# Loading q in runs for two of six token groups, decaying it as it leaves PSUM, and a new order of steps, in a linear-attention and MLP kernel

## The chip, the cores and the metric

The kernel runs on one core of one Trainium2 chip. The metric is the device time of one execution in microseconds (us), lower is better. The five engines of a core are named as in the profile: PE is TensorE (with PEld for its weight loads), DVE is VectorE, ACT is ScalarE, POOL is GpSimd and SP is SyncE. Each engine executes its own instructions in order and waits on semaphores for the others.

## The reference

Two functions follow each other. The first is causal linear attention with a decay for each head; the second is an MLP with the activation h * tanh(softplus(h)), named Mish in the kernel. Cut to what matters (`pos` counts 0 to 63 inside a block of 64):

```python
# q, k, v: (4, 8, 768, 64) float32; lam: (8,)
Dmask = where(rel >= 0, lam ** rel, 0)              # rel = pos_i - pos_j
for each block of 64 positions:
    intra = ((q @ k.T) * Dmask) @ v
    inter = (q * lam ** (pos + 1)) @ kv_state
    out = intra + inter
    kv_state = lam ** 64 * kv_state + (k * lam ** (63 - pos)).T @ v
x = out as (3072, 512)
h = x @ w_in                                        # (512, 2048)
return (h * tanh(softplus(h))) @ w_out              # (2048, 512)
```

## The kernel before

**Tiling.** The kernel takes 128 positions as one block instead of 64, which gives the same function. There are six groups of positions (n = 0 to 5) and in each four batches (b = 0 to 3); steps are named by n and b. The decay is split into a factor for the key's position (held in the masks `dv` and in `lkt`) and one for the query's position, `lqi`, which multiplies the output of a block at its end: (q k^T masked) v and q times the state are both linear in q, so that it may stand at either place. In group 0 the state is zero and only the first part exists.

**Steps.** For each n and b: `lk`, `lq`, `lv` load k, q and v as float16 by a DMA that POOL issues (L155), with positions on partitions, so that one load consists of 8 heads by 128 rows of 64 numbers. In groups 0 and 1 `pk` and `pq` transpose k and q on PE against the identity `ident` (L313) and DVE or ACT copies the result out of PSUM: `kk` (DVE) and `ek` (ACT) for k, `eq` (DVE) and `ea` (ACT) for q. In groups 2 to 5 the transposes are DMAs of SP (`tk`, `tq`). `sc` computes the scores (L386) into two banks, `mk` multiplies them with the mask (DVE, L392), `yo` or `yt` multiplies with v (L403), `yi` adds q times the state (L418), and `xd` multiplies the output with `lqi` and writes it to `xt`, the input of the MLP (DVE, L423). `kp` (POOL) or `kd` (DVE) makes the decayed keys `ktil`, `pv` and `ra` the new state, `wu` or `wd` its decay.

The MLP of groups 0 and partly 1 is computed directly: `u` (one quarter of w_in by one batch, L610) and `uu` (L627) are matmuls, `mu` and `mv` the activation. All other work of the MLP is by a seven-product scheme: `p` (L573) and `o` (L667) are its matmuls, `ws`, `wt`, `ts` and `gs` its sums of operands (DVE), `ca`, `cc`, `ad`, `c2`, `m` and `oa`, `oc`, `od`, `e` the ways out of PSUM, `st` the stores. `wi` and `wo` load quarters of the two weight matrices.

**Constants at the start.** `ir` is an iota on POOL (`rel`); from it DVE makes `ek` and `eq` (step `ik`), `ei` (`ie`), the identity (`di`) and the causal mask (`dk`). `pl` spreads lam on PE, ACT takes its logarithm (`an`) and `lkt` (`ak`); `dp` copies the logarithms by head pairs (`lnp`, DVE), `dq` and `ai` make `lqi` (DVE, ACT), `al` makes `lbm`. `fk` and `ck` bring the first k, group 0 and batch 0, by SP and ACT. `zz.m` is a filler of PE: matmuls of zeros over m x 128 columns.

**What sets the order.** Nothing is scheduled by rules: the table `ORDER` (L15 to L93) lists all steps, and each engine receives its instructions in that order. What follows @ in a step are the PSUM banks (0 to 7) that it takes. A step that takes a bank waits until the last step that had it is through. The last loop of the kernel (L772) executes the table.

A path for q in "runs" is in the code already, for the groups in `IN_RUNS`, which is empty (L128): `lq` then loads 8 neighbouring rows to one partition, and `pq_` picks the rows apart in its transpose (L327 to L332). Tiles of q, k and v have 8 buffers each (L154).

Of the kernel before, what the change touches and what calls it, by code (L numbers as in the profile page):

```python
# [15 lines left out]
fk lk.1.1 lk.0.1 lq.1.2 lq.0.1 lk.0.3 lq.1.1 lq.0.3 ir lk.0.2 lq.0.0 lv.0.0 lv.0.1 lq.0.2 lv.0.3 z0 ll la  # L16
zz.12@0 pl@1 an ik ak dp dk di zz.57@0 pk.1.1@1 ie dv.1 dq kk.1.1 zz.4@0 pq.1.1@2 pk.0.1@3 kk.0.1 pq.0.1@4
pq.1.2@5 pk.0.3@1 ea.0.1 zz.5@0 pk.0.2@3 sc.0.1@4,6 dv.0 kd.0.2 ek.0.3 ea.1.2 ea.1.1 pq.0.3@1 eq.0.3 zz.7@0
sc.0.3@5,2 mk.0.1.1 mk.0.3.1 ck pk.0.0@1 ek.0.0 pq.0.0@7 ea.0.0 zz.10@0 pq.0.2@1 sc.1.1@7,6 mk.0.3.0 kk.0.2
# [1 line left out]
xd.0.1 wi.1 lv.0.2 wi.0 lk.1.0 wi.2 lq.1.0 lk.1.2 kp.0.1 xd.0.3 mk.0.2.0 mk.0.2.1 zz.4@0 u.0.1.1@2 u.0.1.3@3
lm mu.0.1.1 mu.0.1.3 wi.3 kp.0.3 yo.0.2@1 pv.0.2@4 pv.0.3@2 pv.0.1@3 lk.1.3 lq.1.3 xd.0.0 ra.0.2 xd.0.2
mk.1.1.0 mk.1.1.1 ra.0.1 ra.0.3 kd.0.0 lv.1.0 kp.1.0 lv.1.1 lv.1.2 u.0.1.0@5 u.0.1.2@4 uu.0.0.0.0@1
uu.0.0.0.1@3 uu.0.0.1.0@2 pk.1.0@7 uu.0.0.1.1@6 mv.0.0.0.0 mv.0.0.1.1 mv.0.0.1.0 mv.0.0.0.1 mu.0.1.2
uu.0.2.0.1@1 uu.0.2.1.1@6 mv.0.2.1.1 pk.1.2@2 pq.1.0@3 uu.0.2.0.0@4 mv.0.2.0.1 kk.1.2 mv.0.2.0.0 mu.0.1.0
# [780 lines left out]
```

## Time and profile before

| | us |
|---|---|
| time, median of 3 runs | 200.76 (200.47 to 201.5) |
| the profiled execution | 200.44 |
| its span in the profile | 198.7 |
| PE busy in the span | 188.9 |
| DVE busy | 152.6 |
| POOL busy | 96.4 |
| ACT busy | 94.3 |

The span runs from the first to the last instruction; 1.7 us of the execution lie around it. A busy PE is not one at its peak, since fillers and matmuls in a pipeline count as well. In a timeline row stand the start, the duration, the engine, the line, the operation with what it writes and reads, and the number of instructions that the row takes together; in brackets the idle time before it and what ended it. In a row of the chain of waits stand the start, the duration and what the chain went through. In a row of a group stand the busy time in us and the mean of one in ns, then the idle time before it.

### The profile page before, as it was taken

How to read it: one execution, taken by the hardware profiler on the slowest of the kernel's cores; microseconds unless marked ns; L12 is line 12 of the kernel's file. 1: busy time of each engine (PE TensorE's matmuls, PEld its weight loads, DVE VectorE, ACT ScalarE, POOL GpSimd, SP SyncE). 2: the span in 40 equal slices, each digit the busy share in tenths (PEclk: the TensorE clock that was granted, in tenths of full speed). 3: DMA queues.
4: the chain of work that ended last, by engine and by line, in shares of the span. 5: the costliest groups of instructions: out<-in, count | busy, mean ns of one | idle time of the engine just before them, and what ended most of it. 6: DMA issues, size and time to landing. Idle time of an engine off the chain costs nothing.

```text
span 198.7 us, 5683 instructions
## 1 busy us (share of the span) xinstructions
PE 188.9 (95%) x2398; PEld 160.3 (81%) x2398; DVE 152.6 (77%) x298; ACT 94.3 (47%) x174; POOL 96.4 (49%) x110
## 2 busy tenths in 40 slices
PE   8597999999999998999999999999999999999992
PEld 3264897888888887888888888888888888888881
DVE  0395936999997999859999676999759997686521
ACT  2066227537455131387731659612758236575410
POOL 7999989900990796709930489801342000000000
PEclk9999999999999999999999999999999999999998
DMA  8999999999597299999999369997929104201044
GB/s 89 143 141 175 200 182 159 205 205 150 87 93 90 59 168 167 160 170 112 176 167 60 93 137 133 189 171 153 93 48 143 45 0 139 79 0 56 0 158 162
DMA packets 103228, 24.63 MB, mean 124 GB/s; under 512 B 92834, under 2 KB 103202, under 8 KB 103202
## 3 DMA queue, kind: packets, MB, share of 16 engines
q0 software_dynamic: 78064, 13.51, 88.5%
q1 hardware_dynamic: 24992, 10.69, 25.1%
q8 instruction: 19, 0.31, 0.7%
q14 instruction: 7, 0.06, 0.1%
q10 hardware_dynamic: 146, 0.07, 0.1%
HBM read 27.26 MB, written 6.29 MB: 169 GB/s over the span
## 4 chain that ended last, share of the span: by engine, by line
PE 78%; DVE 10%; POOL 5%; DMA 3%; issue 1%; ACT 1%; POOLq 0%
PE b L667 35%; PE b L573 25%; PE b L627 5%; PE b L403 3%; PE b L386 3%; DMA vn<-in_v_dram 3%; DVE hs L473 3%; POOL qn L155 3%; PE b L418 2%; PE b L610 2%; POOL kn L155 2%; PE b L430 2%; DVE wt L473 1%; DVE ws L473 1%; POOL vn L155 1%
## 5 line engine op out<-in xcount | busy, mean ns | idle before, releaser
L667 PEld LDWEIGHTS <-hs 128*128 128x128 f16 x384 | 37.2, 98 | 4.9 <-issue 0.2
L602 ACT ACTIVATE hsg<-b 128x512 f16<-128x512 f32 x54 | 31.2, 596 | 12.3 <-PE b L573 12.1
L667 PE MATMUL b<-wt,hs 128*128 128x256 f16 x288 | 36.4, 273 | 0.2 <-ACT b L676 0.2
L392 DVE TENSOR_TENSOR sb<-b,dv 128x512 f16<-128x512 f32 x48 | 30.5, 684 | 3.4 <-PE b L386 3.3
L573 PEld LDWEIGHTS <-ws 128*128 128x128 f16 x288 | 28.1, 98 | 3.3
L667 PEld LDWEIGHTS <-hsg 128*128 128x128 f16 x288 | 27.8, 98 | 3.6
L573 PE MATMUL b<-xs,ws 128*128 128x256 f16 x216 | 30.0, 273 | 0.0
L359 POOL TENSOR_TENSOR ktil<-kn,lkt 128x512 f16<-128x512 f16 x17 | 20.7, 1218 | 17.6 <-DMA kn<-in_k_dram 15.7
L667 PE MATMUL b<-wout,hsg 128*128 128x256 f16 x192 | 24.3, 273 | 0.0
L443 POOL TENSOR_TENSOR w<-raw,lbm 128x256 f16<-128x256 f32 x9 | 7.5, 837 | 33.7 <-DVE raw L439 33.7
L573 PEld LDWEIGHTS <-win 128*128 128x128 f16 x216 | 20.9, 98 | 2.6
L155 POOL DMA_DIRECT2D vn<-in_v_dram x24 | 21.9, 923 | 1.3 <-DMA win<-in_moe_w_in_dram 1.1
L155 POOL DMA_DIRECT2D qn<-in_q_dram x24 | 22.1, 934 | 0.1
L155 POOL DMA_DIRECT2D kn<-in_k_dram x23 | 21.3, 939 | 0.8 <-POOLq L790 0.8
L707 ACT ACTIVATE osb<-b 128x512 f32<-128x512 f32 x12 | 7.2, 596 | 28.5 <-PE b L667 28.5
L573 PE MATMUL b<-xt,win 128*128 128x256 f16 x144 | 20.1, 273 | 0.0
L470 DVE TENSOR_TENSOR b<-b,p 128x512 f32<-128x512 f32 x18 | 12.5, 697 | 9.4 <-PE b L573 4.6
L627 PE MATMUL b<-xt,win 128*128 128x256 f16 x160 | 19.1, 273 | 0.0
L627 PEld LDWEIGHTS <-win 128*128 128x128 f16 x160 | 15.3, 98 | 1.9
L634 ACT ACTIVATE hsg<-b 128x512 f16<-128x512 f32 x20 | 11.4, 606 | 11.3 <-PE b L627 11.2
L423 DVE TENSOR_TENSOR xt<-b,lqi 128x512 f16<-128x512 f32 x24 | 15.7, 685 | 1.2 <-PE b L418 1.1
L470 DVE TENSOR_TENSOR c<-b,p 128x512 f32<-128x512 f32 x18 | 12.3, 686 | 5.1 <-PE b L573 5.0
(78 smaller groups left out, 284.7 us busy)
## 6 DMA issues: line engine op xcount, KB each, us to landing
out_dram<-osb SPq DMA_DIRECT2D x23, 256.0 KB, 3.0
qn<-in_q_dram POOLq DMA_DIRECT2D x24, 128.0 KB, 5.7
vn<-in_v_dram POOLq DMA_DIRECT2D x24, 128.0 KB, 4.9
kn<-in_k_dram POOLq DMA_DIRECT2D x23, 128.0 KB, 6.4
win<-in_moe_w_in_dram POOLq DMA_DIRECT2D x4, 512.0 KB, 9.9
wout<-in_moe_w_out_dram POOLq DMA_DIRECT2D x4, 512.0 KB, 9.6
osb<-in_k_dram SPq DMA_DIRECT2D x1, 256.0 KB, 3.0
kraw<-kn SPq DMA_TRANSPOSE x16, 2.5
```

Source lines behind the costliest of these rows:

```text
L155: nc.gpsimd.dma_start(out=to[n, b], in_=rows(t, n, b))
L359: engine.tensor_tensor(out=ktil[n, b], in0=kn[n, b], in1=bc(lkt, 2, D), op=ALU.mult)
L392: nc.vector.tensor_tensor(out=sb[n, b, t], in0=pS[n, b][t], in1=dv[:, t], op=ALU.mult)
L423: nc.vector.tensor_tensor(out=xts(n, b), in0=pO.pop((n, b)), in1=lqi, op=ALU.mult)
L443: nc.gpsimd.tensor_tensor(out=wst[b], in0=raw.pop((n, b)), in1=lbm, op=ALU.mult)
L470: nc.vector.tensor_tensor(out=o, in0=a, in1=b, op=ALU.add)
L473: nc.vector.tensor_tensor(out=o, in0=a, in1=b, op=ALU.subtract)
L573: nc.tensor.matmul(t[:, mi, :], w_half(i, s, mi, kc), x_half(n, i, kc), start=(i in (1, 5) and mi == 0 and kc == 0), stop=(mi == 1 and kc ...
L602: nc.scalar.activation(hidden(n, col - 1, row - 1)[:, 2 * s : 2 * s + 2], src, AF.Mish)
L627: nc.tensor.matmul(ph[n, w, h, f0][:, f, :], win[:, kc, ni * 128 : (ni + 1) * 128], xt[n][:, kc, h * HT : (h + 1) * HT], start=(f == 0 and ...
L634: nc.scalar.activation(hidden(n, h, w // 2)[:, f : f + 2], ph.pop((n, w, h, f0)), AF.Mish)
L667: nc.tensor.matmul(t[:, tb, :], g_half(n, i, ki, tb), o_half(i, ki), start=(i in (1, 5) and tb == 0 and ki == 0), stop=(tb == 1 and ki == ...
```

## The change

Four things are changed together.

1. `IN_RUNS` becomes (0, 1): the eight loads of q for groups 0 and 1 go in runs, 128 partitions of 8 neighbouring rows each, and their eight `pq` become 16 matmuls of 64 columns each into a float32 bank, instead of 4 transposes of 128 columns into a float16 one.
2. A new step `es` replaces the copy of q in group 0: DVE multiplies q with `lqi` as it takes it from PSUM. `lqi` must be there before the scores of group 0.
3. `xa` replaces `xd` in group 0: ACT copies the output from PSUM to `xt`. (A step `xc` that copies on DVE is defined and not used.)
4. The table `ORDER` is new from end to end. Among the kinds of steps, all copies of k in groups 0 and 1 are now `ek` (ACT; before, five of eight were `kk`), `kd` stands six times instead of three and `kp` 14 times instead of 17, `wu` 11 times instead of 9 and `wd` 5 instead of 7, `ea` three times instead of six and `eq` once instead of twice. The products of the MLP are the same in number.

```diff
-fk lk.1.1 lk.0.1 lq.1.2 lq.0.1 lk.0.3 lq.1.1 lq.0.3 ir lk.0.2 lq.0.0 lv.0.0 lv.0.1 lq.0.2 lv.0.3 z0 ll la
-zz.12@0 pl@1 an ik ak dp dk di zz.57@0 pk.1.1@1 ie dv.1 dq kk.1.1 zz.4@0 pq.1.1@2 pk.0.1@3 kk.0.1 pq.0.1@4
...
+fk lq.0.1 lk.1.1 lq.1.2 lk.0.3 lq.0.0 lk.1.0 lq.0.3 ir lk.0.1 lv.0.0 lk.1.2 lq.0.2 lk.0.2 lq.1.0 lv.0.3 ll la
+wi.1 lv.0.2 lq.1.1 lv.0.1 z0 zz.12@0 pl@1 an dp ik ie di dq dk ak ck zz.41@0 pk.0.3@1 kd.1.0 dv.1 zz.13@0
...
-    IN_RUNS = ()
+    IN_RUNS = (0, 1)
...
+    @step
+    def es(n, b):
+        nc.vector.tensor_tensor(out=turned(qraw, "qraw", n, b), in0=pq.pop((n, b)), in1=lqi, op=ALU.mult)
...
+    @step
+    def xa(n, b):
+        nc.scalar.activation(xts(n, b), pO.pop((n, b)), AF.Copy)
```

The first place is POOL's queue from its first load on. `kn`, `qn`, `vn` are tiles of k, q and v (a number tells one tile from the next), and the last figures are the shape that is written. Before:

```order
L155 DMA kn_97<-in_k_dram 128x8x64
L155 DMA kn_99<-in_k_dram 128x8x64
L155 DMA qn_101<-in_q_dram 128x8x64
L155 DMA qn_103<-in_q_dram 128x8x64
L155 DMA kn_105<-in_k_dram 128x8x64
L155 DMA qn_107<-in_q_dram 128x8x64
L155 DMA qn_109<-in_q_dram 128x8x64
L226 ISA
L226 IOTA rel_71 128x128
L155 DMA kn_112<-in_k_dram 128x8x64
```

And with the change:

```order
L171 DMA qn_97<-in_q_dram 128x1x512
L155 DMA kn_99<-in_k_dram 128x8x64
L171 DMA qn_101<-in_q_dram 128x1x512
L155 DMA kn_103<-in_k_dram 128x8x64
L171 DMA qn_105<-in_q_dram 128x1x512
L155 DMA kn_107<-in_k_dram 128x8x64
L171 DMA qn_109<-in_q_dram 128x1x512
L226 ISA
L226 IOTA rel_71 128x128
L155 DMA kn_112<-in_k_dram 128x8x64
```

Seven loads stand ahead of the iota in both; four of them are now loads in runs, before none was.

The second place is VectorE from the making of lqi on. `b` with a number is a PSUM bank, `sb` a masked score, `dv` the mask, `lnp` the logarithms of lam. Before:

```order
L286 TENSOR_TENSOR lqi_80<-ei_73,lnp_79 128x512
L347 COPY kraw_166<-b1_158 128x512
L347 COPY kraw_180<-b3_175 128x512
L266 TENSOR_TENSOR dv_77<-maskT_72,lkt_78 128x512
L359 TENSOR_TENSOR ktil_226<-kn_112,lkt_78 128x512
L335 COPY qraw_239<-b1_234 128x512
L392 TENSOR_TENSOR sb_264<-b6_208,dv_77 128x512
L392 TENSOR_TENSOR sb_266<-b2_247,dv_77 128x512
L392 TENSOR_TENSOR sb_312<-b5_246,dv_77 128x512
```

And with the change, from the first es on, up to the mask behind which the bank of the last transpose ahead of the first u (bank 2) is free:

```order
L360 TENSOR_TENSOR qraw_223<-b3_187,lqi_80 128x512
L364 TENSOR_TENSOR ktil_276<-kn_103,lkt_78 128x512
L397 TENSOR_TENSOR sb_278<-b3_230,dv_77 128x512
L266 TENSOR_TENSOR dv_77<-maskT_72,lkt_78 128x512
L397 TENSOR_TENSOR sb_281<-b2_229,dv_77 128x512
L360 TENSOR_TENSOR qraw_300<-b6_259,lqi_80 128x512
L360 TENSOR_TENSOR qraw_319<-b5_302,lqi_80 128x512
L360 TENSOR_TENSOR qraw_383<-b3_327,lqi_80 128x512
L397 TENSOR_TENSOR sb_424<-b5_365,dv_77 128x512
L397 TENSOR_TENSOR sb_426<-b7_348,dv_77 128x512
L397 TENSOR_TENSOR sb_428<-b2_366,dv_77 128x512
```

The copies of k and q have left VectorE here, and four products with lqi stand ahead of the masks of batches 0, 2 and 1.

The third place is ScalarE up to the first outputs of group 0. Before:

```order
L306 ACTIVATE kn_268<-osb_95 128x512
L343 ACTIVATE kraw_275<-b1_270 128x512
L355 ACTIVATE qraw_282<-b7_277 128x512
L278 ACTIVATE lbm_81<-lnp_79 128x256
L290 ACTIVATE lqi_80<-lqi_80 128x512
L355 ACTIVATE qraw_353<-b1_289 128x512
L223 ACT_TABLE_LOAD
```

And with the change:

```order
L306 ACTIVATE kn_153<-osb_95 128x512
L343 ACTIVATE kraw_204<-b1_167 128x512
L343 ACTIVATE kraw_220<-b2_180 128x512
L290 ACTIVATE lqi_80<-lqi_80 128x512
L278 ACTIVATE lbm_81<-lnp_79 128x256
L223 ACT_TABLE_LOAD
L343 ACTIVATE kraw_292<-b5_249 128x512
```

The exponential for lqi now stands behind two copies of k, ahead of it stood four copies of q and two of k (four of these rows are above the piece of before).

More of the change, by code (lines that the diff above doesn't have):

```diff
@@ L21 @@
[L21 to L25, printed above, removed]
@@ L91 @@
[L91 to L92 removed]
+fk lq.0.1 lk.1.1 lq.1.2 lk.0.3 lq.0.0 lk.1.0 lq.0.3 ir lk.0.1 lv.0.0 lk.1.2 lq.0.2 lk.0.2 lq.1.0 lv.0.3 ll la
+wi.1 lv.0.2 lq.1.1 lv.0.1 z0 zz.12@0 pl@1 an dp ik ie di dq dk ak ck zz.41@0 pk.0.3@1 kd.1.0 dv.1 zz.13@0
+pk.1.0@2 zz.4@0 pq.0.3@3 ek.0.3 pk.1.1@1 zz.3@0 pk.0.1@4 ek.1.0 ai es.0.3 zz.6@0 sc.0.3@2,3 al lm pk.0.0@5
+zz.10@0 pq.0.2@6 kd.0.3 mk.0.3.1 dv.0 mk.0.3.0 zz.6@0 pk.0.2@7 ek.0.0 ek.0.2 ek.1.1 ek.0.1 es.0.2 pq.0.0@5
@@ new lines @@
+mk.1.1.0 kd.1.2 uu.0.0.0.1@4 uu.0.0.0.0@2 uu.0.0.1.1@5 uu.0.0.1.0@6 mv.0.0.0.1 mv.0.0.0.0 mu.0.1.1 mv.0.0.1.0
+mv.0.0.1.1 uu.0.2.1.0@4 uu.0.2.1.1@2 pq.1.3@7 pk.1.3@6 mk.1.2.1 ek.1.3 mu.0.1.2 mv.0.2.1.1 uu.0.2.0.0@1
+mv.0.2.1.0 eq.1.3 yt.1.0@7 yt.1.1@6 yi.1.0 sc.1.3@5,3 yi.1.1 pv.1.0@2 xd.1.0 xd.1.1 wo.1 wo.0 lq.2.1 lk.2.3
+wo.3 gs.0.1.0.4 gs.0.3.0.4 ra.1.0 mk.1.3.0 mk.1.3.1 ws.1.1 ws.2.1 kp.1.1 kd.1.3 wo.2 lk.2.1 lq.2.0
+uu.0.2.0.1@4 uu.1.2.0.0@7 uu.1.0.0.0@6 uu.0.3.0.1@2 uu.0.3.0.0@5 uu.0.3.1.1@3 mv.1.0.0.0 mv.0.2.0.0 mv.0.3.0.1
@@ new lines @@
+mv.1.2.0.0 mv.0.3.0.0 yt.1.2@6 pv.1.3@1 yt.1.3@2 yi.1.2 yi.1.3 uu.0.3.1.0@7 p.1.3.1@5 xd.1.2 xd.1.3 ts.1.1
+ra.1.3 ws.3.1 ts.1.2 ts.1.3 ca.1.3@6 mv.0.3.1.0 mv.0.2.0.1 wt.1.0 ws.4.1 wt.1.1 uu.1.0.1.0@2 uu.1.0.0.1@1
+mv.1.0.1.0 p.1.2.5@7 cc.1.2 p.1.2.1@4 uu.1.0.1.1@2 p.1.3.5@7 lk.2.0 lq.2.2 lk.2.2 lv.2.1 kp.2.1 lq.2.3 tk.2.0
+ca.1.2@0 mv.0.3.1.1 gs.0.1.4.8 p.1.2.6 mv.1.0.0.1 uu.1.2.1.1@3 mv.1.2.1.1 mv.1.0.1.1 cc.1.3 uu.1.2.0.1@1
+mv.1.2.0.1 p.1.3.2 p.1.3.6 p.1.2.2 m.1.2.11 gs.0.2.0.4 o.0.1.0@3 uu.1.2.1.0@2 m.1.3.11 mv.1.2.1.0 ws.1.0
@@ new lines @@
+p.2.3.3 sc.3.1@4,0 p.2.3.7 gs.2.1.0.2 m.2.1.21 m.2.3.12 ad.2.2@3 p.2.2.3 m.2.2.12 m.2.1.22 o.2.1.0@6 wu.2.2
+lq.3.0 gs.2.2.0.2 p.2.2.7 gs.2.4.0.2 c2.2.3 e.1.22 kp.3.2 c2.2.2 gs.2.1.2.4 m.2.3.22 m.2.2.22 mk.3.1.0
+mk.3.1.1 o.2.1.1 p.2.3.4 o.1.4.0 p.2.2.4 oa.2@5 m.2.2.21 o.1.4.1 m.2.3.21 pv.3.1@3 yt.3.1@4 tq.3.0 tq.3.2
+gs.2.3.0.2 gs.2.1.6.8 gs.2.1.4.6 gs.2.3.4.6 gs.2.2.6.8 kp.3.0 lk.3.3 wu.2.1 kp.3.3 sc.3.0@0,2 yi.3.1
+gs.2.2.4.6 ra.3.1 gs.2.3.6.8 gs.2.2.2.4 gs.2.4.6.8 mk.3.0.0 mk.3.0.1 wd.3.1 xd.3.1 gs.2.4.4.6 st.0.22 tk.3.3
@@ L93 @@
+gs.5.3.4.6 gs.5.4.2.4 oc.5 o.5.2.0 od.5@7 gs.5.4.6.8 ed.4.21 gs.5.4.4.6 o.5.7.0 st.4.12 st.3.21 st.4.21
+st.4.22 o.5.3.0 o.5.7.1 o.5.3.1 o.5.2.1 e.5.22 o.5.4.0 o.5.4.1 ed.5.210 ex.5 st.5.22 e.5.12 e.5.11 ey.5 sy.5
+st.5.12 st.5.11 st.5.210 sx.5
 """
@@ L423, in xd, with xc @@
         nc.vector.tensor_tensor(out=xts(n, b), in0=pO.pop((n, b)), in1=lqi, op=ALU.mult)
+    @step
+    def xc(n, b):
+        nc.vector.tensor_copy(xts(n, b), pO.pop((n, b)))
+    @step
+    def xa(n, b):
+        nc.scalar.activation(xts(n, b), pO.pop((n, b)), AF.Copy)
     @step
```

125 lines of the change are left out of this document (55 added, 70 removed).

## The prediction

> **What bounds the kernel now.** I read the page first, for which engine is full and where, then the table of windows, then the chain of waits and the timeline of the first 21 us.
>
> ```profile
> span 198.7 us, 5683 instructions
> PE 188.9 (95%) x2398; PEld 160.3 (81%) x2398; DVE 152.6 (77%) x298; ACT 94.3 (47%) x174; POOL 96.4 (49%) x110
> PE   8597999999999998999999999999999999999992
> PEclk9999999999999999999999999999999999999998
> ...
> 0.00:20.00 20.00, 15.12 (x181) 8.24 (x183) 9.93 (x24) 8.12 (x14) 18.93 (x27) 1.00 1.70 137
> 20.00:195.03 175.03, 173.75 (x2221) 152.04 (x2219) 142.41 (x274) 85.89 (x159) 77.52 (x84) 1.00 1.10 122
> 195.03:198.70 3.67, 0.00 (x0) 0.00 (x0) 0.29 (x1) 0.28 (x1) 0.00 (x0) 0.78 0.48 162
> ```
>
> In a row of windows stand the length, then the busy time of PE, PEld, DVE, ACT and POOL, then the granted clock. TensorE is the bound, but only from about 20 us: from there to its last matmul (195.03) it is busy 173.75 of 175.03 us, so that it idles 1.3 us in all. Before 20 us its 15.1 us are largely dummy matmuls of zz and single small steps, while POOL is busy 18.9 of 20. So the end of the kernel is the moment at which TensorE gets real work without a break, plus the work left then, plus a tail that the change leaves as it is. The prediction is about the first of these three, and then about the second.
>
> The break-free stretch begins with the first u. What released it:
>
> ```profile
> 12.09 5.55 DMA vn<-in_v_dram
> 17.68 0.41 PE b L403 x8
> 18.49 0.69 DVE sb L392
> ...
> 12.09 0.98 POOL L155 DMA_DIRECT2D vn<-in_v_dram  x1
> 12.95 0.87 POOL L184 DMA_DIRECT2D win<-in_moe_w_in_dram  x1
> 13.69 1.01 POOL L155 DMA_DIRECT2D vn<-in_v_dram  x1
> ...
> 19.75 1.29 DVE L423 TENSOR_TENSOR xt<-b,lqi 128x512 f16<-128x512 f32 x2
> 20.49 1.95 PE L610 MATMUL b<-xt,win 128*128 128x128 f16 x32
> ...
> L184 POOL DMA_DIRECT2D win<-in_moe_w_in_dram x1: 868/868/868, 13.0 to 13.0; - x1
> ...
> DMA to landing us min/median/max: 7.2/7.2/7.2
> ```
>
> Two things end together at u (20.49): the chain load of v, yo, scores, mask, yo, xd (19.75 + 0.69 = 20.44), and the first quarter of win, issued at 12.95 and landed 7.2 us later, at 20.15. Both hang on POOL's queue of loads, so an earlier start needs both earlier.
>
> **The change part by part.** *The loads of q.* A plain load has 1024 pieces (8 heads by 128 rows, from the code), a load in runs 128, a quarter of win 512.
>
> ```profile
> 3.17 1.75 POOL qn L155 x2
> ...
> 7.55 0.33 POOL L226 IOTA rel<- 128x128 f32 x1
> 7.74 0.96 POOL L155 DMA_DIRECT2D kn<-in_k_dram  x1
> ...
> DMA to landing us min/median/max: 3.8/3.9/4.0
> ```
>
> Plain loads leave POOL 0.875 us apart, the one of win is followed after 13.69 - 12.95 = 0.74 us. A line through these two gives 0.64 us for 128 pieces. Bounds: 0.11 us if time went by pieces alone (an eighth of 0.875), and 0.875 if it did not depend on them. I take 0.64, nearest to the row with the fewest pieces. Ahead of the first win there are now 14 loads instead of 13, eight plain and six in runs: 1.26 + 8 x 0.875 + 6 x 0.64 + 0.34 for the iota = 12.4 us instead of 12.95. The first loads land 3.9 us after their issue, the v of 12.09 took 5.55: by then 1.6 us of backlog had gathered, and win's 7.2 us contain it. Without it win lands at 12.4 + 5.6 = 18.0, with it at 19.6. Pieces fall from 13,312 to 8,960 ahead of win while bytes rise by one load, so I take the lower end with a small remainder, 18.2.
>
> *The constants and the first scores.* The iota is now behind seven loads of which four are in runs: 1.26 + 3 x 0.875 + 4 x 0.64 = 6.4 instead of 7.55.
>
> ```profile
> 8.04 0.83 DVE L274 COPY lnp<-lnb 64x4 f32<-64x4 f32 x2
> 9.04 0.65 DVE L249 TENSOR_SCALAR ident<-rel 128x128 f16<-128x128 f32 x1
> 9.84 0.38 PE L313 MATMUL b<-ident,kn 128*128 128x128 f16 x4 [2.19 <-DVE ident L249]
> ...
> 13.49 1.90 DVE L392 TENSOR_TENSOR sb<-b,dv 128x512 f16<-128x512 f32 x3
> 15.75 0.63 ACT L290 ACTIVATE lqi<-lqi 128x512 f32<-128x512 f32 x1
> ```
>
> The two copies of lnp (0.83 us) stand ahead of the iota's wait instead of behind it, so the identity is there about 1.9 us earlier, at 7.8. The first transposes need only that and their loads. The k of group 1, batch 0 (sixth load, issue 4.9, landing 8.9) is transposed by 9.3 and copied by ScalarE by 9.9, then lqi follows (0.63): 10.6. There the new product es can begin, and from there VectorE has eleven instructions up to the mask that frees the bank for the last transpose ahead of u. Three masks take 1.90 us, 0.61 apart, so eleven take 6.7 us: 17.3. The es of batches 2 and 0 wait for q and k loads issued at 9.4 and 10.0 (landing 13.3 and 13.9), which I put at 0.6 us more: 17.9. One transpose of q (0.4) follows, and u starts at 18.4, with win there since 18.2. **The start moves by 18.4 - 20.5 = -2.1 us.**
>
> *Software for the turn.* pq of groups 0 and 1 has 16 matmuls of 64 columns on 128x64 weights instead of 4 of 128x128, eight times.
>
> ```profile
> 10.73 0.49 PEld L313 LDWEIGHTS <-qn 128*128 128x128 f16 x8
> 59.44 0.44 PE L430 MATMUL b<-vn,ktil 128*64 128x64 f16 x16
> 71.16 0.57 PE b L386 x32
> 135.52 0.50 PE b L403 x16
> ```
>
> The old form takes 0.24 (half of 0.49). Sixteen matmuls of the new shape, pv, take 0.33 to 0.44, and the same weights with 128 columns (yo) 0.50; the matmuls of the new form accumulate into strided columns of a float32 bank, which no row shows. I take 0.42, +0.18 each, within +0.09 to +0.33. Six of the eight lie before or at the start, where TensorE waits anyway; two lie behind it, +0.4.
>
> *What is left at the start.* Before u, the old order has done 5 pk, 6 pq, 5 sc and 3 yo; the new one 7 pk, 6 pq, 4 sc and 1 yo. So one sc (0.28) and two yo (0.50) come later, two pk (0.48) earlier: +0.3, and with the turns **+0.7 us of work behind the start.**
>
> *es, xa and the copies.* es does on q what xd did on the output, four for four.
>
> ```profile
> L423 DVE TENSOR_TENSOR xt<-b,lqi 128x512 f16<-128x512 f32 x24 | 15.7, 685 | 1.2 <-PE b L418 1.1
> L359 DVE TENSOR_TENSOR ktil<-kn,lkt 128x512 f16<-128x512 f16 x3 | 2.1, 684 | 0.0
> L347 DVE COPY kraw<-b 128x512 f16<-128x512 f16 x5 | 2.0, 415 | 4.6 <-PE b L313 4.6
> L355 ACT ACTIVATE qraw<-b 128x512 f16<-128x512 f16 x6 | 3.5, 595 | 2.7 <-PE b L313 2.7
> L699 DVE COPY osb<-b 128x512 f32<-128x512 f32 x5 | 3.4, 688 | 2.2 <-PE b L667 2.2
> L707 ACT ACTIVATE osb<-b 128x512 f32<-128x512 f32 x12 | 7.2, 596 | 28.5 <-PE b L667 28.5
> ```
>
> VectorE keeps four of 685 ns (es for xd), loses five copies of k (415 ns each) and takes three more ktil products from POOL (684 each, two of them counted in the chain above); its other copy of q, in group 1, now reads float32, for which its 688 ns float32 copy is the nearest row. All in all +0.3 us on an engine that is 77% busy. ScalarE gains four xa and five kraw copies and loses three of qraw, 6 x 0.6 = 3.6 us; its cover is the idle half of its span (47% busy), and up to 20 us it is busy 8.1 of 20. That it reads float32 no slower than float16 is in its two rows. I cost these at nothing beyond the chain above. If ScalarE were late with an xa, u would wait for it directly, at most 0.6 us for one instruction.
>
> *The rest of the order.* Stretches behind the start are as full of TensorE work as before; idle there was 1.3 us, and I leave it so, with 0 and 2.6 us as ends.
>
> **Sum:** -2.1 + 0.7 = -1.4 us. Against the profiled execution, 200.44 us (span 198.7 and 1.7 around it), that is 199.0; against the median of the three runs, 200.76, it is 199.4. I say 199.3.
>
> **The rivals.** *The start stays tied to win.* If a load in runs costs POOL as much as a plain one, 14 loads put win's issue at 1.26 + 14 x 0.875 + 0.34 = 13.85 and its landing, with 5.6 to 7.2 us, at 19.5 to 21.0. With u at 20.2 the sum is -0.3 + 0.7 = +0.4: 201.2. The same happens more mildly if the backlog stays (19.6: -0.9 + 0.7, 200.6). For it speaks that no row has so few pieces; against it, that 512 pieces leave POOL sooner than 1024. The Trainium skill, "DMA: Bandwidth & Descriptors", section "Anatomy of one DMA — SWDGE (gpsimd) path", holds the generation of descriptors for small: one "can emit a lot of descriptors before the incremental cost shows up". By that rule the issue would not shorten and this rival would hold; the 0.13 us between the two rows speak against it, though only at 512 pieces and more.
>
> *Slower: the clock.* The dummy stream before the identity is cut from 57 to 41.
>
> ```profile
> 2.91 4.74 PE L296 MATMUL b<-kzero 128*128 128x512 f16 x15
> ...
> 5.44 0.15 PEld L296 LDWEIGHTS <-kzero 128*128 128x128 f16 x1 [0.28 <-issue]
> 5.87 1.45 PEld L296 LDWEIGHTS <-kzero 128*128 128x128 f16 x7 [0.28 <-issue]
> ```
>
> Weight loads of this stream are 0.43 us apart until 5.87, then 0.21: the clock doubled after 4.9 us of work that began at 0.99. The new stream is 4 matmuls shorter and ends near 6.7. If the clock were lost between there and u, TensorE would again need 4.9 us at half speed, of which 2.4 are lost behind the start: 199.4 + 2.4 = 201.8. The point that decides is whether the gap to the first transpose (6.7 to 7.9) and the later ones stay short; the old gap from 7.65 to 9.84 did not cost the clock. The Trainium skill, "TensorE: Matmul & The Clock Gate", Part 1, lets the clock fall after an idle window of about 3.4 us, which by my times is not reached.
>
> *Given back.* The new order waits later for what it gained: idle behind the start doubles, or an operand of group 1 is not there. -1.4 + 1.3 gives 200.6. That TensorE idles only 1.3 us there in an order made with the same steps speaks against it; that every step behind the start stands in a new place speaks for it.
>
> **How the numbers follow.** Start as forecast (17.9 to 19.0, 198.8 to 199.9): 0.5. Tied to win, 200.6 to 201.2: 0.25. Given back, 200.6: 0.15. Clock, 201.8: 0.1. A measurement of this kernel tells about 0.5%, 1.0 us, from no change, so "faster" begins below 199.76: most of the first case and a little of the others, 0.5. "Slower", above 201.76: the clock, and the bad ends of two others, 0.12. The rest, 0.38. For the range I take the first case with fewer waits below (idle 0.8 less, 198.0) and up to win's landing above, 201.2.
>
> **What would show it.** Right: POOL's loads of q about 0.64 apart from the next; iota near 6.4; first kn transposes near 7.9; VectorE without idle from about 10.6 to 17.9; u at 18.4; last matmul near 193.6. Wrong: q loads 0.87 us long in steps (first rival); weight loads of the dummies 0.43 apart after 7 us or a granted clock below 1.00 (clock); u early but TensorE idle over 2 us behind it (given back); 16 matmuls of pq taking over 0.6 us.

## The result and the profile after

| | kernel before | changed kernel |
|---|---|---|
| time, median of the runs side by side (us) | 200.62 (200.45 to 201.5) | 204.06 (203.5 to 204.72) |
| the profiled execution, its span (us) | 200.44, 198.7 | 204.50, 202.7 |
| start of the first u (us) | 20.49 | 22.01 |
| span less that start (us) | 178.2 | 180.7 |

The changed kernel is slower: 1.0148 times the time of before, 95% interval 1.0107 to 1.0190. The forecast was 199.3 us with a range of 198.0 to 201.2. Of the 4.0 us that the span grew, 1.5 lie ahead of the first u and 2.5 behind it. Executions in a slower state, which a few runs had, are left out of all medians and ratios.

The page of the changed kernel, with span, busy times and granted clock:

```profile
span 202.7 us, 5893 instructions
PE 193.7 (96%) x2499; PEld 162.8 (80%) x2499; DVE 150.8 (74%) x293; ACT 97.2 (48%) x180; POOL 90.3 (45%) x109
PE   8689989999999999999999999999999999999992
PEclk9969999999999999999999999999999999999999
```

TensorE is as full as before, and fuller by name (193.7 us busy for 188.9), but the clock dips in the third slice, between 10 and 15 us. That is where the start was lost. The timeline of the start and of the two later waits, engines together (start, duration, engine, line; in brackets the idle time before it and what ended it):

```profile
2.91 0.63 POOL L171 DMA_DIRECT2D qn<-in_q_dram  x1
6.65 0.26 POOL L226 IOTA rel<- 128x128 f32 x1
8.30 0.40 PE L313 MATMUL b<-ident,kn 128*128 128x128 f16 x4 [0.91 <-DMA kn<-in_k_dram]
10.80 0.61 PE L313 MATMUL b<-ident,kn 128*128 128x128 f16 x4 [1.40 <-DMA kn<-in_k_dram]
12.48 0.81 POOL L184 DMA_DIRECT2D win<-in_moe_w_in_dram  x1
12.95 0.69 DVE L360 TENSOR_TENSOR qraw<-b,lqi 128x512 f16<-128x512 f32 x1 [0.80 <-ACT lbm L278]
22.01 1.07 PE L623 MATMUL b<-xt,win 128*128 128x128 f16 x16
27.27 0.22 PE L408 MATMUL b<-sb,vn 128*64 128x128 f16 x1 [1.00 <-issue]
117.00 0.60 PE L586 MATMUL b<-xt,win 128*128 128x256 f16 x4 [0.87 <-DVE raw L452]
```

POOL did what was forecast: a load in runs takes it 0.63 us, the iota comes at 6.65 (forecast 6.4), win is issued at 12.48 (12.4). The loads did not follow. In the chain of waits the sixth load ends at 5.04 + 5.71 = 10.75 instead of the 8.9 forecast, the first es begins at 12.95 instead of 10.6, u at 22.01 instead of 18.4:

```profile
5.04 5.71 DMA kn<-in_k_dram
10.76 0.05 issue
10.80 0.61 PE b L313 x4
...
15.68 0.57 PE b L332 x16
```

And the first quarter of win, from the list of that line (issue, then the time to landing), landed at 12.48 + 8.0 = 20.5, where the forecast had 18.2:

```profile
L184 POOL DMA_DIRECT2D win<-in_moe_w_in_dram x1: 812/812/812, 12.5 to 12.5; - x1
DMA to landing us min/median/max: 8.0/8.0/8.0
```

### The profile page after: what moved, and what is told of

It is laid out like the page before. It is cut to its first block, busy times and chain, and to the rows that moved or that the text cites. A ratio compares the mean times of both kernels' runs of the same rounds, so it can differ in the third digit from the quotient of the medians.

```text
span 202.7 us, 5893 instructions
## 1 busy us (share of the span) xinstructions
PE 193.7 (96%) x2499; PEld 162.8 (80%) x2499; DVE 150.8 (74%) x293; ACT 97.2 (48%) x180; POOL 90.3 (45%) x109
## 4 chain that ended last, share of the span: by engine, by line
PE 83%; DVE 9%; DMA 3%; POOL 2%; issue 2%; ACT 0%; POOLq 0%
PE b L680 32%; PE b L586 26%; PE b L640 9%; PE b L391 3%; DMA kn<-in_k_dram 3%; DVE sb L397 2%; PE b L332 2%; PE b L408 2%; DVE xt L428 2%; PE b L623 2%; PE b L296 2%; PE b L423 2%; PE b L443 1%; PE b L313 1%; DVE xs L486 1%
## 5 line engine op out<-in xcount | busy, mean ns | idle before, releaser
L615 ACT ACTIVATE hsg<-b 128x512 f16<-128x512 f32 x54 | 30.8, 597 | 17.6 <-PE b L586 17.3
L456 POOL TENSOR_TENSOR w<-raw,lbm 128x256 f16<-128x256 f32 x11 | 8.0, 735 | 42.7 <-DVE raw L452 42.7
L680 PE MATMUL b<-wout,hsg 128*128 128x256 f16 x192 | 24.9, 273 | 0.0
L364 POOL TENSOR_TENSOR ktil<-kn,lkt 128x512 f16<-128x512 f16 x14 | 15.5, 1118 | 14.2 <-DMA kn<-in_k_dram 14.2
L586 PE MATMUL b<-xt,win 128*128 128x256 f16 x144 | 21.0, 273 | 0.9 <-DVE raw L452 0.9
L593 ACT ACTIVATE b<-b 128x512 f32<-128x512 f32 x18 | 10.5, 586 | 23.1 <-PE b L586 19.8
L640 PE MATMUL b<-xt,win 128*128 128x256 f16 x160 | 18.8, 273 | 0.0
L155 POOL DMA_DIRECT2D qn<-in_q_dram x16 | 14.6, 924 | 2.6 <-DMA wout<-in_moe_w_out_dram 1.8
L647 ACT ACTIVATE hsg<-b 128x512 f16<-128x512 f32 x20 | 10.9, 603 | 8.7 <-PE b L640 8.7
L428 DVE TENSOR_TENSOR xt<-b,lqi 128x512 f16<-128x512 f32 x20 | 13.0, 681 | 2.5 <-PE b L423 2.5
```

The source lines that it names most:

```text
L155: nc.gpsimd.dma_start(out=to[n, b], in_=rows(t, n, b))
L364: engine.tensor_tensor(out=ktil[n, b], in0=kn[n, b], in1=bc(lkt, 2, D), op=ALU.mult)
L428: nc.vector.tensor_tensor(out=xts(n, b), in0=pO.pop((n, b)), in1=lqi, op=ALU.mult)
L456: nc.gpsimd.tensor_tensor(out=wst[b], in0=raw.pop((n, b)), in1=lbm, op=ALU.mult)
L586: nc.tensor.matmul(t[:, mi, :], w_half(i, s, mi, kc), x_half(n, i, kc), start=(i in (1, 5) and mi == 0 and kc == 0), stop=(mi == 1 and kc ...
L593: nc.scalar.activation(ph[n, s, "b"], ph[n, s, "a"], AF.Copy)
```

## The experiments

Most kernels are the changed one with one thing undone. The first u and the span less its start are from each one's trace; medians are compared with the kernel before of the same series (201.11 in the first series, 200.86 to 201.50 in the later ones).

| run | median us | ratio to before, 95% | first u | span less u |
|---|---|---|---|---|
| e1 plain loads | 201.57 | 1.0036 [1.0003, 1.0068] | 21.82 | 178.1 |
| e2 old order, runs | 206.15 | 1.0256 [1.0183, 1.0329] | 20.68 | 184.2 |
| e3 no wait for the sixth load | 203.73 | 1.0135 [1.0068, 1.0201] | 22.38 | 180.3 |
| e4 more filler | 202.17 | 1.0058 [1.0026, 1.0091] | 20.99 | 178.9 |
| e5 plain loads, more filler | 201.89 | 1.0062 [1.0027, 1.0097] | 21.82 | 178.4 |
| e6 win fifth | 201.40 | 1.0036 [1.0006, 1.0067] | 13.02 | 185.8 |
| e7 old order, es and xa | 209.03 | 1.0402 [1.0356, 1.0447] | 24.33 | 183.6 |
| e8 ktil behind the sums | 203.68 | 1.0135 [1.0087, 1.0182] | 21.86 | 179.3 |
| e9 old decay, new order | 206.79 | 1.0266 [1.0222, 1.0310] | 24.34 | 180.9 |
| e10 single dummies | 205.72 | 1.0231 [1.0159, 1.0303] | 22.00 | 181.9 |
| e11 win fifth, u first | 201.86 | 1.0030 [0.9991, 1.0068] | 11.95 | 188.4 |
| e12 old order, runs, ktil on VectorE | 202.55 | 1.0067 [1.0026, 1.0109] | 22.57 | 179.4 |
| e13 old decay, more filler | 205.47 | 1.0185 [1.0116, 1.0254] | 22.10 | 181.6 |
| e14 more filler, ktil behind the sums | 202.32 | 1.0048 [1.0022, 1.0073] | 21.29 | 178.8 |

### The loads in runs: e1, e2

```diff
-    IN_RUNS = (0, 1)
+    IN_RUNS = ()
```

> The changed kernel with IN_RUNS = (): new order, es and xa stay, loads and turns of q as before. Theory bytes (loads follow each other at about 0.87 us per 128 KB written, whatever their pieces, so runs bring no load in earlier): the k of group 1, batch 0 still lands at 10.3 to 11.0 us, u starts at 21.0 to 22.0, and the time is 203.0 to 203.8 since only the turns become cheaper (0.57 to 0.24 us each, two of them behind the start). Theory runs (the loads in runs themselves delay the landings): the k lands before 9.6, u starts before 20.7, time below 202.

e2 is the opposite: the kernel before with `IN_RUNS = (0, 1)`.

> The kernel before with IN_RUNS = (0, 1) and nothing else. Theory bytes: the first loads land within 0.5 us of before (the fourth at 7.5 to 8.5), u stays at 20.2 to 21.0, and the longer turns add 0.3 to 1.0 us: 200.9 to 201.7. Theory runs: the fourth load lands 1 us or more later than 8.03, u after 21.3, time above 202. If loads in runs did help: u before 20.0, time below 200.4.

Without runs the changed kernel takes 201.57, 2.5 us less (2.3 by the ratios). Its first u is hardly earlier, but for another reason: it now waits for win alone, in the timeline of TensorE of e1:

```profile
21.82 1.07 PE L623 MATMUL b<-xt,win 128*128 128x128 f16 x16 [1.54 <-DMA win<-in_moe_w_in_dram]
```

What the runs cost lies behind the start, 180.7 against 178.1. The landing of the theory of bytes came true: the sixth load, a plain one in both kernels, is issued at 5.7 in e1 and lands 4.6 us later, at 10.3; in the changed kernel it is issued 0.7 us earlier and lands 0.4 us later. In the old order the runs cost 5.0 us, most of it in a gap that e12 takes up. Neither theory had these waits.

### The clock: e3, e4, e5

e3 takes the wait for the sixth load out of VectorE's and ScalarE's queues ahead of the first es:

```diff
-pk.0.3@1 kd.1.0 dv.1 zz.13@0
+pk.0.3@1 dv.1 zz.13@0
...
-ek.0.3 pk.1.1@1 zz.3@0 pk.0.1@4 ek.1.0 ai es.0.3
+ek.0.3 ai pk.1.1@1 zz.3@0 pk.0.1@4 ek.1.0 es.0.3 kd.1.0
```

> The changed kernel; kd.1.0 moved behind es.0.3 on VectorE, and lqi's exponential ahead of ek.1.0 on ScalarE, so that neither waits for the sixth load ahead of the first es. Theory head of line (the first es waits for that load and shifts the whole chain up to u): es starts at 11.9 to 12.2 instead of 12.95, u 0.6 to 1.0 us earlier than 22.0, time 203.1 to 203.6. If the later loads or the clock set u: es earlier, u and the time unchanged within 0.3 us.

It fell: es began at 13.34, 0.4 us later than in the changed kernel, and u at 22.38. The queues of VectorE and ScalarE were not the bound, since TensorE itself stands behind that load and then turns q at half clock. The 0.4 us are not the edit's: in this execution the sixth load took 6.1 us to land instead of 5.71. The timeline of VectorE of e3:

```profile
13.34 0.69 DVE L360 TENSOR_TENSOR qraw<-b,lqi 128x512 f16<-128x512 f32 x1 [3.85 <-PE b L332]
```

e4 fills TensorE's idle time with dummies instead:

```diff
-zz.41@0 pk.0.3@1 kd.1.0 dv.1 zz.13@0
+zz.53@0 pk.0.3@1 kd.1.0 dv.1 zz.41@0
```

> The changed kernel with zz.41 made 53 and zz.13 made 41, so that TensorE is kept busy between 7.4 and 10.8 us. Theory clock (the half clock at 10.6 to 14.0 us delays the turns): granted clock 1.00 from the warm-up on, u 0.5 to 1.0 us earlier, time 203.1 to 203.7. If the clock is hidden behind the loads: full clock, u and time unchanged within 0.3 us.

u starts at 20.99, a full us earlier (in e14, with the same dummies, 0.7), and the time falls by 1.9 us to 202.17 (1.8 by the ratios). So the half clock is real, and more dummies are the cure. Not all of the gain is the clock's: the two traces differ by 2.8 us, of which 1.0 is the start, 0.8 a shorter stall at 26 us and 0.9 the wait at 117 us, which e4 doesn't have; both are taken up below. When the half clock comes can be read from the table of windows. The trace shows the granted clock changing at points 3.41 us apart; a row has start and end, the length, then TensorE's busy time, and the granted clock third from the end. The window ahead of the dip and the dip in the changed kernel:

```profile
7.19:10.60 3.41, 1.30 (x10) 0.53 (x8) 1.47 (x4) 1.42 (x3) 3.41 (x5) 1.00 1.69 143
10.60:14.02 3.42, 3.21 (x33) 2.53 (x34) 2.37 (x4) 2.55 (x4) 3.42 (x5) 0.50 2.04 153
```

The same window in the kernel before:

```profile
5.97:9.38 3.41, 1.68 (x9) 0.64 (x7) 1.43 (x6) 0.30 (x1) 3.40 (x5) 1.00 2.21 141
```

And in e12, further below:

```profile
7.97:11.39 3.42, 1.41 (x25) 1.00 (x25) 1.81 (x5) 0.00 (x0) 3.42 (x5) 1.00 1.66 164
```

The two windows nearest to the edge, in e8, which had half the clock for the next, and in e7, which kept it:

```profile
7.66:11.08 3.42, 1.52 (x13) 0.81 (x13) 1.40 (x5) 0.98 (x2) 3.42 (x6) 1.00 1.88 161
...
6.82:10.24 3.42, 1.65 (x12) 0.74 (x10) 2.30 (x8) 0.30 (x1) 3.41 (x5) 1.00 2.27 145
```

The kernel before, with TensorE busy for 1.68 of 3.41 us, kept the full clock for the next window, and so did e5 with 1.69 and e7 with 1.65. The changed kernel with 1.30 and e12 with 1.41 had half of it, as had e1 (1.19), e3 (1.14), e8 (1.52) and e9 (1.24). e4, with 3.24 us there, kept it. The points lie elsewhere in each execution (a window begins at 7.19 in the changed kernel, at 7.66 in e8), so that one kernel can lose the clock in one execution and keep it in the next. In e12 three of ten executions have a mean granted clock of 0.992, as its trace has with one window at half, and took 203.42 to 203.78 us; the other seven, at 0.998 and more, took 200.82 to 202.82.

e5 is e1 and e4 together.

> The changed order with es and xa, with plain loads of q and their transpose (no software turn), and 52 more dummy matmuls of 128 columns ahead of the first scores, so that TensorE isn't idle there. Theory (the loads in runs bring nothing at landing and cost TensorE 0.57 instead of 0.24 us a turn and some stalls; the half clock costs 1 us of start): both gains add up. The plain loads gave 201.57 and the filler alone 202.18 beside 201.27 for the kernel before; together 1.0 to 1.9 us less than plain loads alone, 199.7 to 200.6, ratio 0.992 to 0.997, granted clock full from about 6 to 7 us on. Rival (the start is tied to the landing of the first quarter of win, at 21.8 us in the run with plain loads, whatever the clock): the start of the first u stays at 21.5 or later and the time within 0.5 us of 201.6.

The theory fell and the rival held to the letter: with the clock whole u still starts at 21.82, on win's landing (1.43 us of wait in its row). With plain loads the clock has slack; with runs win lands at 12.48 + 7.6 = 20.1 in e4, 1.7 us earlier, and the clock decides. So the runs do bring win earlier than plain loads in the same order, by about the 1.3 us that POOL issues it earlier. The new order takes that away, since it puts one more load ahead of win.

### Stalls for instructions: e10

The gap at 26.06 of the changed kernel ends with "issue". Each dummy of 512 columns is written as four of 128:

```diff
-            for n in [4] * (m // 4) + [1] * (m % 4):
+            for n in [1] * m:
```

> The changed kernel; each dummy matmul of 512 columns is written as four of 128 columns on the same zeros, so that TensorE's program has about 75 matmuls and 75 weight loads more ahead of the first u, and the same columns to multiply. Theory (the stall of 1.2 us at 26.06 comes from fetching TensorE's instructions: in four kernels it stands at the same count of instructions from the start, 705, whatever step is there, and it ends 2.2 to 2.4 us after the start of a 16 KB instruction transfer): the eight matmuls of yo at which TensorE stood still run without the stall; a stall, if any over 0.4 us, stands at that count again, now some 150 instructions earlier in the program. Rival (that step itself waits for something that the profile doesn't show, a bank or an operand): the stall of 0.8 to 1.2 us stays at the same matmuls of yo behind the first u.

The table of windows up to the start of the stall, with the counts of matmuls and of weight loads in the first two brackets, in the changed kernel:

```profile
0.00:26.05 26.05, 22.75 (x349) 14.47 (x351) 15.49 (x32) 11.61 (x20) 23.98 (x34) 0.93 1.47 156
```

In e4:

```profile
0.00:24.72 24.72, 23.09 (x349) 14.16 (x351) 14.77 (x31) 11.60 (x20) 23.04 (x33) 1.00 1.47 154
```

In e10, up to its first stall and up to its second:

```profile
0.00:23.70 23.70, 19.78 (x350) 17.29 (x351) 13.15 (x27) 10.03 (x18) 22.18 (x33) 0.93 1.49 152
0.00:28.70 28.70, 24.24 (x478) 21.13 (x479) 15.60 (x33) 13.18 (x23) 24.36 (x35) 0.94 1.52 158
```

In the kernel before, up to a stall that it has at 79 us:

```profile
0.00:78.90 78.90, 73.23 (x989) 58.93 (x989) 61.22 (x111) 32.89 (x60) 58.95 (x68) 1.00 1.48 144
```

The timeline of TensorE where the two stalls of e10 end:

```profile
24.27 0.36 PE L391 MATMUL b<-qraw,kraw 64*64 64x128 f16 x12 [0.55 <-issue]
...
30.74 0.25 PE L443 MATMUL b<-vn,ktil 128*64 128x64 f16 x4 [1.97 <-issue]
```

With 150 instructions more ahead of it, the stalled yo runs through, and the stall stands at an earlier step, sc, but at the same count: 349 + 351 = 700, in e10 701, and 700 in e3, in e8 and in e4, where it stands at a turn of q. A second one stands at 957, which is 256 more, and the one of the kernel before at 1978, within two of five times 256 further than 700; e7 has one of 1.0 us at 1978 too. The step does not matter, the count does. The list of DMA queues has one for instructions, with one transfer between 28.38 and 29.35 in e10 and none in the 5.4 us ahead of it; the stall ended at 30.74. So TensorE ran out of instructions at the end of a block of 256. In the changed kernel it went through that block from 21.1 us (445 matmuls and weight loads by then) to 26.05, 5 us, in e10 through the next in 4.3. The Trainium skill, "Runtime: NRT & Kernel Launch", section "Instruction fetch mechanics", has the blocks of 16 KB and 256 instructions, and the traces agree; it calls the cost of crossing one "mostly hidden", and here it was 0.2 us (e4) to 2.0 us of idle time. What delays the transfer was not tried. The turn by software, with 32 instructions for 8, is what makes the stretch dense; without it, in e1 and e5, there is no such stall.

### VectorE beside GpSimd: e8, e12, e14

e8 moves GpSimd's ktil of group 4 in the table:

```diff
-kp.4.0 kp.4.2 kp.4.3 kp.4.1 wu.3.2 lv.4.1 wu.3.3 lv.4.0
+wu.3.2 wu.3.3 kp.4.0 kp.4.2 kp.4.3 kp.4.1 lv.4.1 lv.4.0
```

> The changed kernel; on GpSimd alone, the two updates wu of group 3 stand ahead of the four ktil products of group 4 instead of between and behind them, so that these products start only when VectorE has done the sums xs and raw of group 3 (about 113.8 to 117 us). Theory (VectorE's float16 sums and GpSimd's ktil products hold each other up: 0.41 us became 0.8 to 1.26 us each while they ran side by side, and TensorE waited 0.87 us for raw): the sums take 0.41 each again, the gap of TensorE near 116 us vanishes, the total falls by 0.6 to 1.1 us against the changed kernel (204.06), to 203.0 to 203.5. Rival (the sums were slow for another reason, or TensorE would wait there for something else next): the sums stay at 0.8 us or more, or the gap stays over 0.7 us, and the total stays within 0.4 us of 204.06.

The timelines of VectorE and GpSimd in the changed kernel:

```profile
113.83 1.59 DVE L486 TENSOR_TENSOR xs<-xt 128x512 f16<-128x512 f16 x2
115.35 1.26 DVE L486 TENSOR_TENSOR xs<-xt,xs 128x512 f16<-128x512 f16 x1
...
113.96 4.73 POOL L364 TENSOR_TENSOR ktil<-kn,lkt 128x512 f16<-128x512 f16 x4 [4.42 <-DMA kn<-in_k_dram]
```

And in e8:

```profile
113.33 0.75 DVE L486 TENSOR_TENSOR xs<-xt 128x512 f16<-128x512 f16 x2
114.00 0.42 DVE L486 TENSOR_TENSOR xs<-xt,xs 128x512 f16<-128x512 f16 x1
...
115.62 4.04 POOL L364 TENSOR_TENSOR ktil<-kn,lkt 128x512 f16<-128x512 f16 x4
```

Side by side, a sum took 0.8 to 1.26 us and a ktil 1.18; apart, 0.4 and 1.01. Other traces bear this out: the sums take 0.4 us in e1, e4 and e10 as well, where the table of GpSimd is that of the changed kernel but its ktil happen to begin behind them (in e4 the last sum ends at 113.2 and the first ktil begins at 114.11), and 0.8 to 1.26 us in e3 and e13, where they begin beside them. TensorE's wait near 116 us is gone in e8, and its profile is 1.5 us shorter. The time does not show it: the median fell by 0.4 us (0.3 by the ratios), which the spread of single executions covers (202.97 to 204.32) and which is what the rival had for the total.

e12 tries the same where it is large, in e2:

```diff
-tq.2.2 kp.2.3 lv.2.1 kp.2.0
+tq.2.2 kd.2.3 lv.2.1 kd.2.0
```

> The kernel before with loads in runs for groups 0 and 1 and the software turn (206.15, with a gap of TensorE of 3.8 us at 55 us), and two ktil products of group 2 given to VectorE behind its sums wt, hs, instead of GpSimd beside them. Theory (VectorE's float16 sums and GpSimd's ktil products hold each other up: two sums of wt took 4.12 us instead of 1.29): the two sums take 1.3 us again, the gap at 55 us falls below 1.2 us, the total falls by 2 to 3.5 us, to 202.7 to 204.2. Rival (the sums are slowed by something else, as the transfers of wout that land then, or VectorE is late anyway): sums stay above 2.5 us, or the gap above 2.5 us, the total within 1 us of 206.

VectorE and TensorE at that place in e2:

```profile
48.95 4.12 DVE L473 TENSOR_TENSOR wt<-wout 128x1024 f16<-128x1024 f16 x2
...
58.99 0.60 PE L573 MATMUL b<-xs,ws 128*128 128x256 f16 x4 [3.52 <-DVE b L470]
```

In e12:

```profile
49.74 2.33 DVE L473 TENSOR_TENSOR wt<-wout 128x1024 f16<-128x1024 f16 x2
...
57.28 0.60 PE L573 MATMUL b<-xs,ws 128*128 128x256 f16 x4 [1.04 <-DVE b L470]
```

GpSimd at that place in the kernel before:

```profile
49.43 3.43 POOL L359 TENSOR_TENSOR ktil<-kn,lkt 128x512 f16<-128x512 f16 x1 [9.41 <-DMA kn<-in_k_dram]
```

The time fell by 3.6 us, to 202.55: the theory, with a little more than its size, though the sums still took 2.33, beside a ktil and an update that stayed on GpSimd. Part of the gain is the clock: in e2 TensorE was busy for 1.36 of the 3.41 us from 57.11, around the gap, and had half the clock for the next 3.41; in e12 it had the full clock there. In the kernel before, the two engines meet as well, and there GpSimd loses: a single ktil takes 3.43 us, beside sums of 0.69 us of 1024 columns, and TensorE doesn't wait. Which of the two is slow differs between runs in which both start at other times; what decides it was not tried. The Trainium skill, "GPSIMD Engine Reference", section "1. Specifications", lists an access to the on-chip memory that GpSimd shares with VectorE; these rows agree.

e14 puts e4 and e8 together.

> The changed kernel with both repairs: the clock kept whole by 52 more dummies, and GpSimd's ktil products of group 4 behind the updates of group 3. Theory (half clock, instruction stall, VectorE beside GpSimd and the turns' 0.7 us are all of the loss): first u at 21.0, no gap near 116 us, a stall of at most 0.5 us at the 700th matmul and weight load; total 201.3 to 202.2, 0.3 to 0.8% above the kernel before, which is what the turns and the later start leave. Rival (more was lost in places not yet seen): total above 202.8.

202.32, 0.1 us above the theory's range and below the rival's. It is no faster than e4 alone, in whose trace the wait near 116 us is gone already. Behind its first u no wait of TensorE is longer than 0.2 us, so that no third loss of size is left in TensorE's waits.

### The decay: e7, e9, e13

e7 is the kernel before with es and xa in the places of the copies and of xd, and `ai` ahead of the first es.

> The kernel before, its order and its plain loads, with one part of the change alone: the decay is taken by VectorE as q of group 0 leaves PSUM (es for the copies of q), and ScalarE copies the outputs (xa for xd); the exponential of lqi moves ahead of the first es. Theory (es and xa only move a multiplication of 685 ns from one place of VectorE's chain to another and cost nothing by themselves): within 0.5% of the kernel before, ratio 0.995 to 1.005, first u within 0.6 us of 20.5. Rival (es puts 0.69 us of VectorE and the wait for lqi on the path of the first scores, which a copy by ScalarE beside it did not): first u 1 to 2 us later, ratio above 1.005.

The rival, and more: 8.2 us slower, u at 24.33. In its trace the fourth es stands in VectorE's queue behind masks whose scores stand in TensorE's behind a yo that waits for v; it begins at 20.08, and TensorE falls to half clock from 20.48 to 27.30; later VectorE and GpSimd meet at 50 us again. So this prices a place in a queue that doesn't suit es, and not es itself.

e9 is the opposite in the new order, `ea` and `xd` for `es` and `xa` of group 0; e13 adds the dummies of e4.

> The changed kernel (loads in runs, new order) with the decay where it was before: q of group 0 is copied by ScalarE (ea for es) and the output takes the factor on VectorE (xd for xa), at the same places of the order. Theory (in the new order es and xa are neutral: VectorE has four products of 0.69 us either way, the start hangs on the loads, on the late turn and on the half clock): first u within 0.7 us of 22.0, total 203.0 to 205.0. Rival (es is what makes the start late, since scores wait for VectorE and for lqi): first u at 21.2 or earlier and the total 0.8 us or more below 204.

> The changed kernel with the decay where it was (ea and xd for es and xa) and with the 52 more dummy columns-of-128 that kept the clock whole in the changed kernel (202.18, first u at 20.99). Theory (the 2.7 us that the old decay cost in the new order were mostly a second stretch at half clock, 9.8 to 16.6 us, that the late scores brought with them): with the clock whole, first u at 20.8 to 21.8 and the total within 0.8 us of 202.2. Rival (ScalarE's queue with six copies in a row, and VectorE's factor ahead of u, hold the scores back by themselves): first u at 22.3 or later, total 203.2 or more.

Neither came out as its theory said, and e9 went the other way than its rival too. Without es and xa the changed kernel is 2.7 us slower and e4 3.3 us (2.4 and 2.6 by the ratios), with the clock whole in both kernels of the second pair. e13's total is the rival's; its first u, at 22.10, lies between the two. The timeline of TensorE in e13 shows where:

```profile
18.25 0.91 PE L391 MATMUL b<-qraw,kraw 64*64 64x128 f16 x32 [0.76 <-ACT qraw L355]
24.73 1.05 PE L623 MATMUL b<-xt,win 128*128 128x128 f16 x16 [0.18 <-DVE xt L428]
28.12 1.05 PE L623 MATMUL b<-xt,win 128*128 128x128 f16 x16 [1.11 <-DVE w L449]
```

Scores wait for ScalarE, which has six copies in a row there, and the later u for VectorE's factor and the masks ahead of it. The start is 1.1 us later than in e4, and the span behind it 2.7 longer; 0.87 us of these are a wait for raw at 118 us, where VectorE and GpSimd meet again, 1.3 are in the last two rows above. The order was made for es and xa, so this too prices the places in it, not the old decay by itself.

### A start at 13 us: e6, e11

e6 has plain loads, es and xa, the first quarter of win as the fifth load, and the batches one after the other; e11 also moves the products with win ahead of group 1's scores.

```diff
+fk lk.0.3 lq.0.3 ir lv.0.3 wi.1 lq.0.0 lk.0.1 lq.0.1 lv.0.0 lv.0.1 lk.0.2 lq.0.2 lv.0.2 ll la wi.0 lk.1.0
...
+sc.0.3@2,4 dv.0 mk.0.3.1 mk.0.3.0 zz.12@0 pk.0.0@5 ek.0.0 al lm zz.16@0 yo.0.3@6 xa.0.3 kd.0.3
...
```

> Plain loads, es and xa as in the changed kernel; the loads are issued in the order in which one batch after the other needs them (k, q and v of batch 3, then the first quarter of win as the fifth load, then the other batches, group 1 behind the second quarter of win), and the steps of TensorE up to the fourth product with win follow that order. Theory (a load lands about 0.9 us after the one ahead of it, whatever its pieces, a quarter of win 2.6 to 4 us after): k, q, v land at 5.2, 6.1, 7.0 to 7.6 and win at 9.6 to 11.6; the first u starts by 12 us, about 10 us earlier than in the changed kernel, and three of the first four u are done where the changed kernel has its first. Two us of real work each replace dummies and idle: the last matmul comes 3 to 6 us earlier than with plain loads in the changed order, total 195.5 to 199. Rival (win lands some 7 us after its issue because a large load takes that long by itself, or the transfers as a whole are the bound, so that the operands of the later steps now come late by as much): win not before 13 us, or TensorE idle over 3 us between 12 and 35 us, and the total stays at 200 or above.

> As the run with win as the fifth load (plain loads, first u at 13.0 us, 201.40), with the rest of the products with win's first and third quarters moved ahead of the turns and scores of group 1, whose loads land at 21 to 30 us. Theory (there TensorE lost some 2 us between 24 and 34 us waiting for q of group 1 and VectorE's masks, with products ready to run): useful work done by 40 us rises by 1 to 2 us against that run, the total is 199.4 to 200.6, 0 to 1.2 us below the kernel before. Rival (by 35 to 40 us everything hangs on the transfers, which move no more bytes in this order): useful work by 40 us the same within 0.5 us, total 201 to 202.

win landed 6.6 us after its issue at 4.29, at 10.9 (in e11 7.3, at 11.6), and u began at 13.02 and at 11.95, 9 to 10 us earlier than in the changed kernel. Yet the totals are those of e1: of the 8.8 us that e6 starts ahead of e1, 7.7 are lost behind it (185.8 for 178.1). The timeline of TensorE in e6 says for what:

```profile
15.08 0.42 PE L392 MATMUL b<-qraw,kraw 64*64 64x128 f16 x16 [0.34 <-DVE qraw L361]
...
25.72 0.40 PE L314 MATMUL b<-ident,qn 128*128 128x128 f16 x4 [0.50 <-DMA qn<-in_q_dram]
```

And in e11:

```profile
34.74 0.38 PE L313 MATMUL b<-ident,qn 128*128 128x128 f16 x4 [1.59 <-DVE sb L397]
```

Of the rivals the totals came true, not the conditions: in e6 win landed before 13 us, and TensorE idled 2.1 us between 12 and 35 us, not over 3. TensorE's busy time less its dummies, up to 40 us, is 22.6 us in e5, 24.9 in e6 and 24.0 in e11: of the 9 to 10 us of earlier start 1 to 2 are left by then, and e11 does less than e6, where its theory had 1 to 2 us more. The rows above show what TensorE waits for in the first 35 us: loads, and VectorE's products and masks. That these set the pace in whatever order the loads come is the reading that fits; no run takes them away. No version that was run beats the kernel before.

## Why the prediction was wrong

- **POOL's side was right.** 0.64 us for a load in runs (measured 0.63), iota 6.4 (6.65), win issued at 12.4 (12.48). The Trainium skill, "DMA: Bandwidth & Descriptors", section "Anatomy of one DMA — SWDGE (gpsimd) path", would have left the issue as it was; the row of 0.63 beside 0.90 for a plain load says otherwise.
- **The failed step is the landing.** "The first loads land 3.9 us after their issue" and "Without it win lands at 12.4 + 5.6 = 18.0", with 18.2 taken. It was assumed that the backlog goes with fewer pieces, and that the loads ahead of it take 3.9 us as before. Win does not land in 5.6 us without a queue ahead of it either: as the fifth load it took 6.6 us in e6 and 7.3 in e11. The wait moved into the transfers: issued faster, the sixth load took 5.71 us instead of the 4.0 put down (4.6 with plain loads, in e1), and win 8.0, more than the 7.2 of before. This moves win to 20.5 and the first es by 1.9 us of its 2.35. In the kernel before no backlog had gathered step by step either: the loads up to the twelfth took 3.8 to 4.6 us, and only the v ahead of win 5.55. Of the 3.6 us by which u came later than forecast (22.01 for 18.4, where the terms add up to 18.3), 1.0 is the clock by e4; with the clock whole, e4 still has the sixth load at 10.7 for 8.9 and the q of batch 2 at 14.8 for 13.3.
- **The clock, a rival at 0.1, came about.** The point of decision, "whether the gap to the first transpose (6.7 to 7.9) and the later ones stay short", was the right place; but the test used an idle window of 3.4 us, after the Trainium skill, "TensorE: Matmul & The Clock Gate", Part 1. The runs lost the clock with TensorE busy for up to 1.52 of 3.41 us. The rival's price of 2.4 us, from 4.9 us at half speed, was too high: in the changed kernel one window of 3.42 us was at half, and it cost 1.0 us of the start by e4.
- **Work behind the start, +0.7, has the right size, in part by luck**: 178.9 in e4 against 178.2. A turn took 0.57 us and not 0.42, which adds 0.3 us for two; against it, the stall of 0.6 us that the kernel before has at 79 us is not in e4.
- **"I leave it so, with 0 and 2.6 us as ends"**, of the waits behind the start: 2.5 - 0.7 = 1.8 us came on top. Beside e4, which has the 0.7 alone, these are the stall for instructions (1.0 instead of 0.2 us) and VectorE beside GpSimd (0.9); 0.1 us is not accounted for. "Given back", with 1.3, had nearly the size, not the causes.
- **"I cost these at nothing", of es and xa**, was wrong: in this order they save 2.4 to 3.3 us. Without them the new order would be slower still.

What stays open: why win's landing grew by more than the lag of the loads ahead of it (8.0 us behind a v that took about 5.3), and what holds an instruction transfer back.

## What to carry to other kernels

A faster issue moves a landing only as far as the transfers follow: read the time from issue to landing as a quantity that grows when issues come closer together, not as a constant. Where TensorE waits in the first 15 us, count its busy share in stretches of 3.4 us, and fill what is under half. And an early first product is worth nothing if the operands behind it come at the old pace: ask what the engine would do next.

## What the runs showed of the hardware

- The clock halved after a window of 3.41 us in which TensorE was busy for 0.76 (e7, from 17.06) to 1.52 us (e8), in nine traces, and stayed whole after 1.65 (e7, from 6.82), 1.68 (the kernel before) and 1.69 (e5). The kernel before stands just above that edge.
- TensorE stops at ends of blocks of 256 instructions when many small matmuls stand in a row: 0.2 to 2.0 us idle, at counts of 700, 957 and 1978 matmuls and weight loads.
- VectorE's float16 sums and GpSimd's products hold each other up by a factor of up to 3.3 (1.26 for 0.42 us, 3.43 for 1.04), and which of the two is slow differs from run to run.
